# Weights from float64 to float32 by moving bits: three VectorE operations in place of five or six

## The chip, the cores and the metric

One core of a Trainium2 chip. The metric is the device time of one execution in microseconds (us), the median over runs. A kernel is called faster or slower where its time differs by more than 2% from that of the kernel before, else the same.

## The reference

Attention with normalised queries and keys, then a feed-forward block with a softmax-weighted activation. All inputs are made as float32, but the two weight matrices are multiplied by a float64 scalar, so they arrive as **float64**:

```python
# attention: batch 8, 12 heads, 448 positions, head size 64
q_n, k_n = rmsnorm(q, g_q), rmsnorm(k, g_k)
attn = softmax(q_n @ k_n.T / sqrt(64));  o = attn @ v
# feed-forward on x = o reshaped to (3584, 768); d_ff = 1024
h = x @ w_in                                   # w_in  768 x 1024, float64
e = exp(h - max(h));  sm = e / (sum(e) + 1e-9)
solu = h * sm
ln = (solu - mean) / sqrt(var + 1e-6) * g_ln
out = ln @ w_out                               # w_out 1024 x 768, float64
```

## The kernel before

Each float64 weight is read as a pair of 32-bit words, `lo` and `hi`, and put together as a float32. This is done in 28 pieces (12 of `w_in` with 128x512, then 16 of `w_out` with 128x384), each in four stages. The stages are not run at once: the kernel's program is a list of **units** (four matmuls of scores, the values, the sums, a feed-forward half), and after each unit every piece under way advances by one stage. So conversion is strewn between the steps of attention.

```python
def load_w(step):      # one piece to SBUF as [128, n, 2] 32-bit words, two buffers
def convert_w(step, raw):
    lo, hi = raw[:, :, 0], raw[:, :, 1]
    def fields():      # VectorE
        nc.vector.tensor_scalar(tmp[:, 1], hi, 0xFFFFF, None, OP.bitwise_and)                              # L467
        nc.vector.tensor_scalar(e, hi, 20, 0x7FF, OP.logical_shift_right, OP.bitwise_and)                  # L468
    def scale():       # ScalarE
        nc.scalar.activation(m, tmp[:, 1], AF.Copy, scale=2.0 ** -20, bias=1.0)                            # L471
        nc.scalar.activation(ei, ei, AF.Relu, bias=m896)                                                   # L472
    def join():        # VectorE
        nc.vector.scalar_tensor_tensor(m, lo, 2.0 ** -52, m, OP.mult, OP.add)                              # L475
        nc.vector.tensor_scalar(ei, ei, 255.0, 2.0 ** 23, OP.min, OP.mult)                                 # L476
        nc.vector.scalar_tensor_tensor(e, hi, 0x80000000, e, OP.bitwise_and, OP.bitwise_or)                # L477
    def product():
        if dst is w_in: nc.gpsimd.tensor_tensor(dst[:, c, cols], m, e.bitcast(FP32), OP.mult)              # L481
        else: nc.vector.scalar_tensor_tensor(dst[:, c, cols], m, gcol[...], e.bitcast(FP32), ...)          # L484
    return [fields, scale, join, product]
...
def rsqrt_seed(n):     # start of the inverse root of the norms; ss is a tile that the matmuls L529 write
    nc.scalar.activation(d["y"], d["ss"], AF.Ln, scale=1.0 / D, bias=eps)                                  # L536
    nc.vector.tensor_scalar(d["x"], d["ss"], -0.5 / D, -0.5e-6, OP.mult, OP.add)                           # L537
    nc.scalar.activation(d["y"], d["y"], AF.Exp, scale=-0.5)                                               # L538
...
def add(n, kc):        # sums of the exponentials E
    if kc == 1: nc.gpsimd.tensor_tensor(d["es"], d["E"][:, 0], d["E"][:, 1], OP.add)                       # L584
    else:       nc.vector.tensor_tensor(d["es"], d["es"], d["E"][:, kc], OP.add)                           # L586
...
for n in range(N):     # N = 48 head pairs; one pass is one period
    ...
    unit(lambda: scores(n, 0));  qk_transpose(n + 1);  later(1, lambda n=n: gain(n + 1))
    unit(lambda: scores(n, 1));  fold_sums(n + 2);     later(1, lambda n=n: rsqrt_seed(n + 2))
    ff(0); unit(lambda: values(n - 1)); unit(lambda: sums(n - 1)); ff(1)
    unit(lambda: scores(n, 2)); unit(lambda: scores(n, 3)); ff(2)
```

Of the kernel before, what the change touches and what calls it, by code (L numbers as in the profile page):

```python
# [9 lines left out]
FP32 = mybir.dt.float32  # L10
U32 = mybir.dt.uint32
I32 = mybir.dt.int32
AX = mybir.AxisListType.X
AF = mybir.ActivationFunctionType
OP = AluOpType
# [351 lines left out]
def fast_path(  # L367
# [7 lines left out]
    out: bass.AP,  # L375
    grow: bass.AP,
    within: bass.AP,
):


# [3 lines left out]
    nc = tc.nc  # L384
    B, H, S, D = q.shape
    DM, DFF = moe_w_in.shape
    P = 128
# [11 lines left out]
    consts = ctx.enter_context(tc.tile_pool(name="consts", bufs=1))  # L399
    loads = ctx.enter_context(tc.tile_pool(name="loads", bufs=2))  # L400
    work = ctx.enter_context(tc.tile_pool(name="work", bufs=2))
    small = ctx.enter_context(tc.tile_pool(name="small", bufs=4))
    ps_h = ctx.enter_context(tc.tile_pool(name="ps_h", bufs=1, space=bass.MemoryType.PSUM))
    ps_t = ctx.enter_context(tc.tile_pool(name="ps_t", bufs=6, space=bass.MemoryType.PSUM))

    ident = consts.tile([P, P], FP32, name="ident")
    ones = consts.tile([P, D], FP32, name="ones")
    fold = consts.tile([P, 2, 2, 32], FP32, name="fold")
    w_in = consts.tile([P, KD, DFF], FP32, name="w_in")
    w_out = consts.tile([P, KF, DM], FP32, name="w_out")  # L410
    gcol = consts.tile([P, KF + 2], FP32, name="gcol")
    mhalf = consts.tile([P, 1], FP32, name="mhalf")
    m896 = consts.tile([P, 1], FP32, name="m896")
    eps = consts.tile([P, 1], FP32, name="eps")

    def setup():

        nc.scalar.add_instruction(
            mybir.InstLoadActFuncSet(
                act_func_set_id=6, name=nc.get_next_instruction_name(), engine=mybir.EngineType.Activation  # L420
            )
        )
        nc.gpsimd.memset(mhalf, -0.5)
        nc.gpsimd.memset(m896, -896.0)
        nc.gpsimd.memset(eps, 1e-6)
        nc.gpsimd.memset(ones, 1.0)
        make_identity(nc, ident)

        nc.gpsimd.memset(fold, 0.0)
        for g in range(4):  # L430
            gs = slice(g * 32, g * 32 + 32)
            for x in range(2):
                nc.gpsimd.tensor_copy(fold[gs, g // 2, x], ident[gs, gs])
        pg = ps_t.tile([P, KF + 2], FP32, tag="t", name="pg")
        nc.tensor.transpose(pg, grow, ident[0 : KF + 2, 0 : KF + 2])
        nc.vector.tensor_copy(gcol, pg)

        nc.vector.tensor_scalar(
            gcol[:, KF : KF + 1], gcol[:, KF : KF + 1], gcol[:, KF + 1 : KF + 2], within, OP.mult, OP.mult
        )  # L440
# [3 lines left out]



    def load_w(step):
        src, _, c, cols = step
        n = cols.stop - cols.start
        raw = work.tile([P, n, 2], U32, tag="raw", name="raw")  # L450
        nc.sync.dma_start(
            raw.rearrange("p n t -> p (n t)"),
            src[c * P : (c + 1) * P, :].bitcast(U32)[:, 2 * cols.start : 2 * cols.stop],
        )
        return raw

    def convert_w(step, raw):

        _, dst, c, cols = step
        n = cols.stop - cols.start  # L460
        lo, hi = raw[:, :, 0], raw[:, :, 1]
        tmp = work.tile([P, 2, n], U32, tag="uT", name="tmp")
        e, m = tmp[:, 0], tmp[:, 1].bitcast(FP32)
        ei = e.bitcast(I32)

        def fields():
            nc.vector.tensor_scalar(tmp[:, 1], hi, 0xFFFFF, None, OP.bitwise_and)  # L467
            nc.vector.tensor_scalar(e, hi, 20, 0x7FF, OP.logical_shift_right, OP.bitwise_and)  # L468

        def scale():  # L470
            nc.scalar.activation(m, tmp[:, 1], AF.Copy, scale=2.0 ** -20, bias=1.0)  # L471
            nc.scalar.activation(ei, ei, AF.Relu, bias=m896)  # L472

        def join():
            nc.vector.scalar_tensor_tensor(m, lo, 2.0 ** -52, m, OP.mult, OP.add)  # L475
            nc.vector.tensor_scalar(ei, ei, 255.0, 2.0 ** 23, OP.min, OP.mult)  # L476
            nc.vector.scalar_tensor_tensor(e, hi, 0x80000000, e, OP.bitwise_and, OP.bitwise_or)  # L477

        def product():
            if dst is w_in:  # L480
                nc.gpsimd.tensor_tensor(dst[:, c, cols], m, e.bitcast(FP32), OP.mult)  # L481
            else:

                nc.vector.scalar_tensor_tensor(  # L484
                    dst[:, c, cols], m, gcol[:, c : c + 1], e.bitcast(FP32), OP.mult, OP.mult
                )

        return [fields, scale, join, product]

    st = {}  # L490
    xTs = {}
# [215 lines left out]
    def unit(f):  # L707
        nonlocal now
        f()
        now += 1  # L710
        due = [x for x in todo if x[0] <= now]
        todo[:] = [x for x in todo if x[0] > now]
        for _, g in sorted(due, key=lambda x: x[0]):
            g()
        feed()
# [6 lines left out]
    W_OUT = 22  # L722
    raws = []
    stages = []
    wdone = 0
    wtarget = 0

# [14 lines left out]
    events = []  # L742
# [32 lines left out]
    with tc.manual_schedule():  # L775
# [17 lines left out]
        at = 0  # L793
# [50 lines left out]
        unit(lambda: None)  # L844
        unit(lambda: values(N - 1))
        unit(lambda: sums(N - 1))
        for _, f in events[at:]:
            unit(f)
        for _ in range(4):
            unit(lambda: None)  # L850


@with_exitstack
def kernel(
    ctx: ExitStack,
    tc: tile.TileContext,
    q: bass.AP,
    k: bass.AP,
    v: bass.AP,
    g_q: bass.AP,  # L860
    g_k: bass.AP,
    moe_w_in: bass.AP,
    moe_w_out: bass.AP,
    moe_g_ln: bass.AP,
    out: bass.AP,
):
    nc = tc.nc
    D = q.shape[3]
    P = 128
    KF = moe_w_in.shape[1] // P  # L870
    gains = ctx.enter_context(tc.tile_pool(name="gains", bufs=1))
    grow = gains.tile([KF + 2, P], FP32, name="grow")
    gg = gains.tile([P, 2, D], FP32, name="gg")
    gmax = gains.tile([P, 1], FP32, name="gmax")
    within = gains.tile([P, 1], FP32, name="within")
    flag = gains.tile([1, 1], I32, name="flag")
    nc.scalar.dma_start(grow[0:KF, :], moe_g_ln.rearrange("(c p) -> c p", p=P))
    for i, g in enumerate((g_q, g_k)):
        for h in range(2):
            nc.scalar.dma_start(grow[KF + i : KF + i + 1, h * D : (h + 1) * D], g.rearrange("(o d) -> o d", o=1))  # L880
    for i, g in enumerate((g_q, g_k)):
        nc.scalar.dma_start(gg[:, i], g.rearrange("(o d) -> o d", o=1).to_broadcast([P, D]))

    nc.vector.tensor_tensor(gg[:, 0], gg[:, 0], gg[:, 1], OP.mult)
    nc.vector.tensor_reduce(gmax, gg[:, 0], AX, OP.max, apply_absolute_value=True)
    nc.vector.tensor_scalar(flag, gmax[0:1], 80.0 / float(D) ** 0.5, None, OP.is_gt)
    nc.vector.tensor_scalar(within, gmax, 80.0 / float(D) ** 0.5, float(D) ** -0.5, OP.is_le, OP.mult)
    fast_path(tc, q, k, v, moe_w_in, moe_w_out, out, grow, within)
    large = nc.values_load(flag[0:1, 0:1], min_val=0, max_val=1)
    with tc.If(large > 0):  # L890
        general_path(tc, q, k, v, g_q, g_k, moe_w_in, moe_w_out, moe_g_ln, out)


# [28 lines left out]
```

## Time and profile before

Median 1110.4 us. To see where time goes I cut the run at the same instruction of each period, the reciprocal on VectorE that belongs to head pair n ("n11" is its start for pair 11):

| stretch | before, us | what sets it |
|---|---|---|
| start to n1 | 51.5 | loads, set-up |
| A: n1 to n11, one `w_in` piece and one head pair in each period | 111.0 | VectorE without a gap, 11.11 a period |
| middle: n11 to n14, nine feed-forward halves fall in it | 86.4 | TensorE, mostly |
| B: n14 to n22, `w_out` pieces | 97.6 | VectorE, mostly |
| n22 to n47 | 620.6 | TensorE |
| n47 to the end | 140.2 | TensorE |

The prediction below shows the main lines. GpSimd in order of time (start, duration, engine, line, operation, idle time before it and its releaser) in a period of A:

```profile
99.30 2.06 POOL L481 TENSOR_TENSOR w_in<-tmp 128x512 f32<-128x512 f32 x1 [2.09 <-DVE tmp L477]
101.31 2.93 POOL L584 TENSOR_TENSOR es<-E 112x896 f32<-112x896 f32 x1
```

VectorE is slower beside both: while L481 runs, the two L586 (from 99.14) take 3.17 us instead of twice 1.08, and the next L467, which starts at 103.25 while L584 still runs, takes 1.28 us, where L468 with the same shape takes 0.41. The prediction calls this the lock; here that is only a name for these longer times. And on TensorE the first feed-forward half:

```profile
164.45 5.40 PE L635 MATMUL h<-w_in,xT 128*128 128x512 f32 x12
```

It starts 1.95 us after n11 and takes 5.40 us.

### The profile page before, as it was taken

Reading aid. Unit: us, or ns where it says so; the run is one execution under the profiler, and the core shown is the slowest. Engines: PE = TensorE matmul, PEld = TensorE weight load, DVE = VectorE, ACT = ScalarE, POOL = GpSimd, SP = SyncE. Lnnn points to the kernel's source line nnn. Section 1 sums busy time; section 2 is a strip of 40 time slices with the busy share of each in tenths; the row PEclk is TensorE's granted clock in tenths of the full one; section 3 lists DMA queues with packets and bytes.
Section 4 is the critical chain, followed back from the end, with each engine's and each line's share of the span. In section 5 each row is a group of like instructions: output and inputs, shape, how many; then the busy total and the mean of one; then the engine's idle time right before and its main releaser. Section 6 shows DMA issues by size and latency. Waiting matters only on the chain.

```text
span 1107.3 us, 10659 instructions
## 1 busy us (share of the span) xinstructions
PE 1035.3 (93%) x3617; PEld 475.6 (43%) x3617; DVE 605.4 (55%) x1018; ACT 370.6 (33%) x773; POOL 240.3 (22%) x155
## 2 busy tenths in 40 slices
PE   3988888888789999999999999999999999999997
PEld 1323233333234444444444444444444444455554
DVE  3999996569997444444444444454446644522300
ACT  3656553235564222222222222332224322311110
POOL 2565651123223111111111011121112211100000
PEclk9899999998989999999999999999999999999999
DMA  7454544014543111111111111121111100000010
GB/s 140 89 122 98 124 87 85 23 39 93 112 88 62 40 40 40 39 32 33 32 37 40 40 40 39 40 51 40 40 39 40 34 23 24 14 15 15 15 44 31
DMA packets 230391, 57.49 MB, mean 52 GB/s; under 512 B 223152, under 2 KB 223160, under 8 KB 230328
## 3 DMA queue, kind: packets, MB, share of 16 engines
q1 hardware_dynamic: 225984, 45.64, 20.9%
q10 hardware_dynamic: 4344, 11.08, 2.6%
q8 instruction: 30, 0.49, 0.2%
q14 instruction: 33, 0.27, 0.1%
HBM read 45.68 MB, written 11.01 MB: 51 GB/s over the span
## 4 chain that ended last, share of the span: by engine, by line
PE 75%; DVE 14%; issue 4%; ACT 3%; DMA 1%; SPq 1%; ACTq 0%; DVEq 0%
PE po L686 27%; PE h L635 26%; PE s L572 9%; PE o L595 9%; DVE es L586 2%; PE pu L676 2%; PE sm L604 2%; DVE tmp L467 2%; DVE qkT L559 2%; DVE tmp L475 1%; SPq L505 1%; DVE r L619 1%; DVE tmp L477 1%; DVE r L617 1%; PE ss L529 1%
## 5 line engine op out<-in xcount | busy, mean ns | idle before, releaser
L635 PE MATMUL h<-w_in,xT 128*128 128x512 f32 x672 | 305.0, 604 | 11.7 <-DVE u L653 11.7
L686 PE MATMUL po<-w_out,uT 128*128 128x384 f32 x896 | 298.0, 489 | 2.9 <-ACT uT L677 2.9
L686 PEld LDWEIGHTS po<-w_out,uT 128*128 128x128 f32 x896 | 168.3, 190 | 132.9 <-issue 15.0
L572 PE MATMUL s<-qkT 64*112 64x448 f32 x768 | 204.6, 584 | 16.9 <-ACT E L576 6.7
L576 ACT ACTIVATE E<-s 112x448 f32<-112x448 f32 x384 | 178.0, 550 | 110.0 <-PE s L572 109.9
L635 PEld LDWEIGHTS h<-w_in,xT 128*128 128x128 f32 x672 | 126.2, 193 | 167.5 <-issue 162.8
L584 POOL TENSOR_TENSOR es<-E 112x896 f32<-112x896 f32 x48 | 110.5, 2301 | 325.2 <-ACT E L576 318.7
L595 PE MATMUL o<-E,v 112*64 112x448 f32 x768 | 163.9, 572 | 1.2 <-DVE xT L621 1.2
L572 PEld LDWEIGHTS s<-qkT 64*112 64x112 f32 x768 | 76.6, 177 | 136.9 <-issue 73.6
L677 DVE COPY uT<-pu 128x512 f32<-128x512 f32 x28 | 19.2, 687 | 187.3 <-PE pu L676 187.3
L586 DVE TENSOR_TENSOR es<-es,E 112x896 f32<-112x896 f32 x96 | 115.1, 1199 | 10.9 <-ACT E L576 7.8
L663 POOL TENSOR_TENSOR he<-he,mhalf 128x1 f32<-128x1 f32 x28 | 21.7, 774 | 379.2 <-DVE he L662 379.2
L549 POOL TENSOR_TENSOR qkn<-qk,ny 128x896 f32<-128x896 f32 x48 | 83.0, 1730 | 81.6 <-DVE ny L544 35.0
L648 ACT ACTIVATE u<-h,hmax 128x1024 f32<-128x1024 f32 x28 | 31.2, 1114 | 207.3 <-DVE hmax L645 207.3
L687 ACT COPY y<-po 128x384 f32<-128x384 f32 x56 | 26.8, 479 | 213.5 <-PE po L686 213.5
L595 PEld LDWEIGHTS o<-E,v 112*64 112x64 f32 x768 | 53.2, 143 | 86.5 <-issue 80.5
L645 DVE TENSOR_REDUCE hmax<-h 128x1 f32<-128x1024 f32 x28 | 34.3, 1224 | 84.3 <-PE h L635 84.3
L604 PE MATMUL sm<-es,ones 112*64 112x448 f32 x192 | 44.8, 544 | 16.0 <-DVE es L586 14.1
L617 DVE STREAM_TRANSPOSE r<-sm 128x448 f32<-128x448 f32 x48 | 31.0, 646 | 45.8 <-PE sm L604 45.8
L524 DVE TENSOR_REDUCE part<-sq 128x28 f32<-128x896 f32 x48 | 51.7, 1076 | 5.9 <-ACT sq L519 5.9
L519 ACT ACTIVATE sq<-qk 128x896 f32<-128x896 f32 x48 | 45.8, 955 | 23.1 <-ACT y L687 11.3
L559 DVE STREAM_TRANSPOSE qkT<-qkn 128x896 f32<-128x896 f32 x48 | 52.9, 1102 | 0.0
(54 smaller groups left out, 578.7 us busy)
## 6 DMA issues: line engine op xcount, KB each, us to landing
qk<-in_q_dram SPq DMA_DIRECT2D x192, 56.0 KB, 2.6
qk<-in_k_dram SPq DMA_DIRECT2D x192, 56.0 KB, 2.4
v<-in_v_dram SPq DMA_DIRECT2D x48, 224.0 KB, 3.0
out_dram<-y ACTq DMA_DIRECT2D x28, 384.0 KB, 2.3
raw<-in_moe_w_in_dram SPq DMA_DIRECT2D x12, 512.0 KB, 4.2
raw<-in_moe_w_out_dram SPq DMA_DIRECT2D x16, 384.0 KB, 3.4
grow<-in_g_q_dram ACTq DMA_DIRECT2D x2, 0.2 KB
grow<-in_g_k_dram ACTq DMA_DIRECT2D x2, 0.2 KB
```

Of the source, the lines that this page charges most:

```text
L519: nc.scalar.activation(d["sq"], d["qk"].rearrange("p s b d -> p (s b) d"), AF.Square)
L524: nc.vector.tensor_reduce(d["part"], d["sq"], AX, OP.add)
L549: nc.gpsimd.tensor_tensor(d["qkn"], d["qk"].rearrange("p s b d -> p (s b) d"), d["y"].rearrange("p b -> p b ()").to_broadcast([P, 2 * NB, ...
L559: nc.vector.transpose(d["qkT"].rearrange("p s t -> p (s t)"), d["qkn"].rearrange("p b d -> p (b d)"))
L572: nc.tensor.matmul(s, d["qkT"][hh, 1, kc * SP : (kc + 1) * SP], d["qkT"][hh, 0, :], start=True, stop=True)
L576: nc.scalar.activation(d["E"][:, kc, h], d["s", h], AF.Exp)
L584: nc.gpsimd.tensor_tensor(d["es"], d["E"][:, 0], d["E"][:, 1], OP.add)
L586: nc.vector.tensor_tensor(d["es"], d["es"], d["E"][:, kc], OP.add)
L595: nc.tensor.matmul(d["o"][h * D : (h + 1) * D, :], d["v"][:, h, kc], d["E"][:, kc, h], start=(kc == 0), stop=(kc == NJ - 1),)
L604: nc.tensor.matmul(d["sm"][h * D : (h + 1) * D, :], ones[0:SP, :], d["es"][:, h], start=True, stop=True)
L635: nc.tensor.matmul(d["h"][:, hs], xTs[m][:, c, i * P : (i + 1) * P], w_in[:, c, hs], start=(c == 0), stop=(c == KD - 1))
L686: nc.tensor.matmul(po, d["uT"][:, c], w_out[:, c, hs], start=(c == 0), stop=(c == KF - 1))
```

## The change

A float32 has three exponent bits fewer than a float64. For weights of ordinary size the float32 is the sign and top exponent bit of `hi`, the rest of `hi` moved up by three, and the top three bits of `lo`. So no arithmetic on exponents is needed: VectorE moves and joins bits, ScalarE gets the three bits out of `lo`. The intent is to relieve VectorE, the bound of the head, and GpSimd. What is given up is the range; so at the end all weights are loaded again, and their smallest and largest high words are checked beside the last units. Where they are out of range, a general path runs. The diff is shortened; comments stand for removed code that is shown above.

```diff
-        def fields():      # two on VectorE
-        def scale():       # two on ScalarE
+        def low_bits():
+            nc.scalar.activation(low, lo, AF.Relu, scale=-(2.0 ** -29), bias=seven)                         # L469
+            nc.scalar.activation(tmp[:, 1].bitcast(I32), low, AF.Copy, scale=-1.0, bias=7.0)                # L470
+        def high_bits():
+            nc.vector.tensor_scalar(t, hi, 3, 0x3FFFFFFF, OP.logical_shift_left, OP.bitwise_and)            # L473
+            nc.vector.scalar_tensor_tensor(t, hi, 0xC0000000, t, OP.bitwise_and, OP.bitwise_or)             # L474
         def join():
-            # three on VectorE
+            o = dst[:, c, cols].bitcast(U32) if dst is w_in else t
+            nc.vector.tensor_tensor(o, t, tmp[:, 1], OP.bitwise_or)                                         # L478
         def product():
-            # w_in: GpSimd, w_out: VectorE
+            if dst is w_out:
+                nc.scalar.activation(dst[:, c, cols], t.bitcast(FP32), AF.Copy, scale=gcol[:, c : c + 1])   # L483
-        return [fields, scale, join, product]
+        return [low_bits, high_bits, join, product]
...
+        again = [load_w(wq[x]) for x in range(2)]          # beside the last units:
+            check_w(x, again[x])                           # two reductions of a piece, L490 and L491
+            check_all()                                    # two transposes on TensorE (L502), some tiny operations
```

In lines of the changed kernel: L536, L537 are now L559, L560; the gain L563 is L586; the transpose L559 is L582; the additions L584, L586 are L607, L609; the feed-forward half L635 is L658. (L559 and L586 thus name other operations in the two kernels.)

More of the change, by code (lines that the diff above doesn't have):

```diff
@@ L377, in fast_path @@
     within: bass.AP,
+    large: bass.AP,
 ):
@@ L412, in fast_path @@
     mhalf = consts.tile([P, 1], FP32, name="mhalf")
-    m896 = consts.tile([P, 1], FP32, name="m896")
+    seven = consts.tile([P, 1], FP32, name="seven")
     eps = consts.tile([P, 1], FP32, name="eps")
@@ L423, in setup @@
         nc.gpsimd.memset(mhalf, -0.5)
-        nc.gpsimd.memset(m896, -896.0)
+        nc.gpsimd.memset(seven, 7.0)
         nc.gpsimd.memset(eps, 1e-6)
@@ L462, in convert_w @@
         tmp = work.tile([P, 2, n], U32, tag="uT", name="tmp")
-        e, m = tmp[:, 0], tmp[:, 1].bitcast(FP32)
-        ei = e.bitcast(I32)
-        def fields():
-            nc.vector.tensor_scalar(tmp[:, 1], hi, 0xFFFFF, None, OP.bitwise_and)
-            nc.vector.tensor_scalar(e, hi, 20, 0x7FF, OP.logical_shift_right, OP.bitwise_and)
-        def scale():
-            nc.scalar.activation(m, tmp[:, 1], AF.Copy, scale=2.0 ** -20, bias=1.0)
-            nc.scalar.activation(ei, ei, AF.Relu, bias=m896)
+        t, low = tmp[:, 0], tmp[:, 1].bitcast(FP32)
@@ L474, in join @@
+        def low_bits():
[4 more added lines that the diff above has]
+            nc.vector.scalar_tensor_tensor(t, hi, 0xC0000000, t, OP.bitwise_and, OP.bitwise_or)
         def join():
-            nc.vector.scalar_tensor_tensor(m, lo, 2.0 ** -52, m, OP.mult, OP.add)
@@ L476, in join @@
-            nc.vector.tensor_scalar(ei, ei, 255.0, 2.0 ** 23, OP.min, OP.mult)
-            nc.vector.scalar_tensor_tensor(e, hi, 0x80000000, e, OP.bitwise_and, OP.bitwise_or)
+            o = dst[:, c, cols].bitcast(U32) if dst is w_in else t
+            nc.vector.tensor_tensor(o, t, tmp[:, 1], OP.bitwise_or)
         def product():
-            if dst is w_in:
-                nc.gpsimd.tensor_tensor(dst[:, c, cols], m, e.bitcast(FP32), OP.mult)
-            else:
-                nc.vector.scalar_tensor_tensor(
-                    dst[:, c, cols], m, gcol[:, c : c + 1], e.bitcast(FP32), OP.mult, OP.mult
-                )
@@ L488, in convert_w, with check_w @@
-        return [fields, scale, join, product]
+            if dst is w_out:
+                nc.scalar.activation(dst[:, c, cols], t.bitcast(FP32), AF.Copy, scale=gcol[:, c : c + 1])
+        return [low_bits, high_bits, join, product]
+    def check_w(x, raw):
+        hi = raw[:, :, 1].bitcast(FP32)
+        nc.vector.tensor_reduce(extent[:, 0, x : x + 1], hi, AX, OP.min, apply_absolute_value=True)
+        nc.vector.tensor_reduce(extent[:, 1, x : x + 1], hi, AX, OP.max, apply_absolute_value=True)
@@ new lines, in check_all @@
+    def check_all():
+        worst = small.tile([P, 2], FP32, tag="mv", name="worst")
+        one = small.tile([1, 2], FP32, tag="one", name="one")
+        pw = ps_t.tile([1, 2, P], FP32, tag="t", name="pw")
+        nc.vector.tensor_reduce(worst[:, 0:1], extent[:, 0], AX, OP.min)
+        nc.vector.tensor_reduce(worst[:, 1:2], extent[:, 1], AX, OP.max)
+        for i in range(2):
+            nc.tensor.transpose(pw[:, i], worst[:, i : i + 1], ident)
+        nc.vector.tensor_reduce(one[:, 0:1], pw[:, 0], AX, OP.min)
+        nc.vector.tensor_reduce(one[:, 1:2], pw[:, 1], AX, OP.max)
+        nc.vector.tensor_scalar(one[:, 0:1], one[:, 0:1], 2.0 ** -15, None, OP.is_ge)
+        nc.vector.tensor_scalar(one[:, 1:2], one[:, 1:2], 122880.0, None, OP.is_lt)
+        nc.vector.tensor_tensor(one[:, 0:1], one[:, 0:1], one[:, 1:2], OP.mult)
+        nc.vector.tensor_scalar(one[:, 1:2], large, -1.0, 1.0, OP.mult, OP.add)
+        nc.vector.tensor_tensor(one[:, 0:1], one[:, 0:1], one[:, 1:2], OP.mult)
+        nc.vector.tensor_scalar(large, one[:, 0:1], -1.0, 1.0, OP.mult, OP.add)
@@ L724, in fast_path @@
     stages = []
+    extent = consts.tile([P, 2, len(wq)], FP32, name="extent")
     wdone = 0
@@ L846, in fast_path @@
         unit(lambda: sums(N - 1))
-        for _, f in events[at:]:
+        last = events[at:]
+        assert len(last) > len(wq) + 1
+        again = [load_w(wq[x]) for x in range(2)]
+        for x, (_, f) in enumerate(last):
             unit(f)
+            if x < len(wq):
+                check_w(x, again[x])
+                if x + 2 < len(wq):
+                    again.append(load_w(wq[x + 2]))
+            if x == len(wq) + 1:
+                check_all()
         for _ in range(4):
@@ L876 @@
     flag = gains.tile([1, 1], I32, name="flag")
+    large = gains.tile([1, 1], FP32, name="large")
     nc.scalar.dma_start(grow[0:KF, :], moe_g_ln.rearrange("(c p) -> c p", p=P))
@@ L885 @@
     nc.vector.tensor_reduce(gmax, gg[:, 0], AX, OP.max, apply_absolute_value=True)
-    nc.vector.tensor_scalar(flag, gmax[0:1], 80.0 / float(D) ** 0.5, None, OP.is_gt)
+    nc.vector.tensor_scalar(large, gmax[0:1], 80.0 / float(D) ** 0.5, None, OP.is_gt)
     nc.vector.tensor_scalar(within, gmax, 80.0 / float(D) ** 0.5, float(D) ** -0.5, OP.is_le, OP.mult)
-    fast_path(tc, q, k, v, moe_w_in, moe_w_out, out, grow, within)
-    large = nc.values_load(flag[0:1, 0:1], min_val=0, max_val=1)
-    with tc.If(large > 0):
+    fast_path(tc, q, k, v, moe_w_in, moe_w_out, out, grow, within, large)
+    nc.vector.tensor_copy(flag, large)
+    other = nc.values_load(flag[0:1, 0:1], min_val=0, max_val=1)
+    with tc.If(other > 0):
         general_path(tc, q, k, v, g_q, g_k, moe_w_in, moe_w_out, moe_g_ln, out)
```

## The prediction

> **What bounds the kernel now.** I read the page first (busy tenths by slice), then busy time by stretch, then the order of time on each engine inside one period of the first stretch, then the waits.
>
> The slices split the run in two:
> ```profile
> PE   3988888888789999999999999999999999999997
> ...
> DVE  3999996569997444444444444454446644522300
> ...
> PEclk9899999998989999999999999999999999999999
> ```
> From slice 13 on (about 340 us) TensorE is busy without a gap and VectorE is half idle. Only the first 340 us, in which the weights are converted, and the very end can answer to this change. Busy time in two stretches of that head:
> ```profile
> 62.00:162.00 100.00, 84.69 (x343) 31.00 (x344) 97.21 (x155) 59.56 (x128) 59.78 (x27) 1.00 0.50 106
> ...
> 248.00:337.00 89.00, 74.80 (x276) 27.77 (x274) 82.61 (x149) 48.53 (x105) 27.61 (x15) 0.87 0.46 95
> ```
> Columns after the length: PE, PEld, DVE, ACT, POOL busy. VectorE has 97 of 100 us in the first (call it A: one head pair and one w_in piece per period) and 83 of 89 in the second (B: eight w_out pieces per five periods). Between them, about 162 to 244 us, lie nine feed-forward halves of 5.2 us each, and TensorE sets the pace. One period of A on VectorE:
> ```profile
> 91.11 1.10 DVE L559 STREAM_TRANSPOSE qkT<-qkn 128x896 f32<-128x896 f32 x1
> 92.14 1.28 DVE L467 TENSOR_SCALAR tmp<-raw 128x512 uint32<-128x512 uint32 x1
> 93.34 0.41 DVE L468 TENSOR_SCALAR tmp<-raw 128x512 uint32<-128x512 uint32 x1
> 93.68 0.17 DVE L537 TENSOR_SCALAR nx<-ss 128x28 f32<-128x28 f32 x1
> ...
> 97.47 0.68 DVE L475 SCALAR_TENSOR_TENSOR tmp<-raw,tmp 128x512 f32<-128x512 uint32 x1
> 98.07 0.42 DVE L476 TENSOR_SCALAR tmp<-tmp 128x512 int32<-128x512 int32 x1
> 98.53 0.69 DVE L477 SCALAR_TENSOR_TENSOR tmp<-raw,tmp 128x512 uint32<-128x512 uint32 x1
> 99.14 3.17 DVE L586 TENSOR_TENSOR es<-es,E 112x896 f32<-112x896 f32 x2
> 102.23 1.10 DVE L559 STREAM_TRANSPOSE qkT<-qkn 128x896 f32<-128x896 f32 x1
> ```
> Column one is the start, column two the duration. There is no gap: VectorE is the bound, the period is 102.23 - 91.11 = 11.12 us. From start to start, conversion takes 1.20 + 0.34 + 0.60 + 0.46 + 0.61 = 3.2 us of it. In the same period ScalarE:
> ```profile
> 92.24 0.67 ACT L563 ACTIVATE qkT<-qkT,gcol 128x448 f32<-128x448 f32 x1 [4.29 <-DVE qkT L559]
> 92.82 0.27 ACT L536 ACTIVATE ny<-ss,eps 128x28 f32<-128x28 f32 x1
> ...
> 93.51 0.63 ACT L471 ACTIVATE tmp<-tmp 128x512 f32<-128x512 uint32 x1 [0.17 <-DVE tmp L467]
> 94.05 0.70 ACT L472 ACTIVATE tmp<-tmp,m 128x512 int32<-128x512 int32 x1
> ```
> The gain L563 waits for the transpose; the logarithm L536 follows it. From the waits of the whole run:
> ```profile
> DVE nx L537 <- ACT ny L536: 71.3, 33, 6.7
> ```
> So VectorE's L537 may not pass L536. In A this wait does not show, because L467 and L468 stand between L559 and L537 and last longer than gain and logarithm.
>
> [...]
> ```profile
> 256.66 2.46 DVE L477 SCALAR_TENSOR_TENSOR tmp<-raw,tmp 128x384 uint32<-128x384 uint32 x1
> ```
> L477 takes 0.56 us when nothing is in its way; here GpSimd's L584 (the first E addition) runs from 256.63 for 2.07 us. In A the lock costs about 0.86 us on L467 (1.28 against 0.41) and 1.0 us on the two L586 (3.17 against 2.16), together 1.9 us a period.[...]
>
> **The change part by part.**
> *VectorE, removed and added.* In A, 3.2 us a period go, 0.86 of them the lock stall on L467, so 2.35 of work. Added: shift-and-mask like L468 (0.46 with the dependent wait), or-in of the top bits like L477 (0.61), join of two unit-stride inputs: L586 is 1.08 us for 896[...], some 0.60 from start to start. Together 1.67, so 0.7 us less work. In B a piece costs now 0.27 + 0.27 + 0.47 + 0.38 + 0.48 + 0.53 = 2.4 us and then 0.27 + 0.48 + 0.47 = 1.2; at 1.6 pieces a period 1.9 us less.
> *GpSimd* loses L481 (1.9 us of w_in product); *ScalarE* keeps two activations a piece and gains the w_out product (0.43 us), and it has room (60 of 100 us).
> *Order.* This decides it. The built programs, compared instruction by instruction, show that in A the two ScalarE operations on the low words now stand between the gain and the logarithm, and on VectorE L537's operation stands directly behind the transpose, ahead of the shift. VectorE then waits: gain 0.58, low words 0.61 + 0.54, logarithm 0.30, and 0.05 to start, so 2.08 us after the transpose ends; the two operations that used to fill this time come after it. The gap is 2.0 us each period.
> *The lock.* GpSimd's E addition starts when ScalarE has done the exponentials, by the present spacing (2.3 us behind the gap's start, then 4.4) some 6.8 us after the transpose's end. VectorE reaches the join at about 7.0 us and the two L586 behind it[...]. One of them waits out GpSimd's 2.05 us: about 1.9 us lost, as much as now, though L481 is gone.
> *Sum for A.* From start to start, what is not conversion takes: transpose 1.03, L537 0.10, row sums L524 1.00, Newton steps 0.54, the divide L617 to L621 2.17, two L586 2.02, together 6.9. With 2.35 of conversion and 1.86 of lock stalls that is 11.1, the period measured, so the account closes. New: 6.9 + 1.67 + gap 2.0 + stall 1.9 = 12.5. Ten periods at +1.35: **+13 us**.
> *B.* Here pieces fall at varying places. In three of eight periods the low words stand before the logarithm (gap 2.0 to 2.5), in the others it is 0.2 to 1.4; the mean of the eight is 1.3. 6.9 + 1.95 (1.6 pieces at 1.22) + 1.3 + a lock stall of 1.4 (the mean of those now seen there) = 11.5 against 12.65 measured (88.5 us in seven periods). **-8 us** over seven.
> *Middle and start.* TensorE sets the middle; start-up gains from L481's absence and loses by the wait: 0 to +1.
> *The check at the end.* The last 32 units hold 28 loads and 56 reductions of 0.55 to 0.69 us, some 34 us. Units average 4.5 us, VectorE is busy 28% there, and a load of 3.4 to 4.2 us with two buffers keeps up, so all of it is hidden behind TensorE. Not hidden: two transposes of the extremes stand on TensorE before the last 10.6 us of output products and wait for two short reductions behind the last copy: about **+1 us**.
> Sum: +13 - 8 + 0.5 + 1 = +6.5 on 1110.4, rounded: **1116 us**.
>
> **Rivals.**
> (1) *The gap does not arise or is filled*, the plain reading of the change: A falls to 6.9 + 1.67 + 1.0 = 9.6, B to 10.2; 15 + 17 us saved, less 1 for the check, 1079 us. For it: VectorE at 97%. Against it: the built order, and L537's wait on L536, which shows 33 times now.
> (2) *The gap arises but the lock stall goes*[...]: A 10.6, B 10.5; 5 + 15 us saved, less 1 for the check, 1092 us. Against it: the spacing above; for it: a shift of only half a microsecond alters who meets whom.
> (3) *TensorE's clock*: in B its granted clock is 0.87, with 12.65 us periods that leave it idle over a third of the time. Should A's longer periods bring that too, scores come later and each period grows by up to 0.5 us: +5, 1121 us.
> (4) *The check is not hidden*: loads fall behind and hold VectorE up before a copy that TensorE needs: 5 to 10 us more, 1124 us. Against it: ten microseconds of output products stand between two uses of the tile h.
>
> **Range and chances.** My sum is 1116; (3) and (4) lie 5 to 8 above it, (2) some 24 below, and each 0.5 us of error in A's period is 5 us. I take 1097 to 1130 for 8 in 10. Faster by over 2% (under 1088) needs rival (1) or nearly: 0.09. Slower by over 2% (over 1132.6) needs A at 13.5 or several costs together: 0.06. Within 2%: 0.85.
>
> **What would show each step.** VectorE busy in A falling from 97 to about 80 of 100 us while its period grows to 12 or more; VectorE idle about 2 us before each operation that L537 is now, released by the logarithm on ScalarE; join or es additions of 2.5 to 3 us beside GpSimd's E addition; B's period near 11.5; TensorE without new gaps after 350 us except 1 us before the last output products. I am wrong if VectorE stays gapless in A with a period under 10.5, or if VectorE holds up TensorE in the last 140 us.

## The result, and the profile after

1124.9 us (1124.4 to 1125.6, 4 runs) against 1110.6 us (1108.0 to 1111.8) on the same chip: **ratio 1.0133**, 95% interval 1.0114 to 1.0152, so "the same" by the 2% rule but surely longer. A ratio here is the mean time of one kernel's fast runs over that of the other's of the same rounds, so not quite the ratio of the medians quoted. The time lies in the range predicted, but the change, +14 us, is more than twice the +6.5 us of the prediction's sum.

The page's busy tenths of VectorE and the granted clock of TensorE, in 40 slices of the changed kernel:

```profile
DVE  3787887455778444444444444444445543555521
PEclk9989998999889999999999999999999999999999
```

VectorE had nines in A (slices 2 to 6) and now has sevens and eights. Busy time by stretch (columns: window and length, then PE, PEld, DVE, ACT, POOL busy, granted clock, DMA share, GB/s), in A and in B (n14 to n22), which has moved later:

```profile
62.00:162.00 100.00, 76.32 (x298) 28.99 (x298) 81.56 (x117) 51.09 (x106) 33.23 (x16) 0.93 0.44 96
272.27:362.78 90.51, 80.69 (x309) 31.62 (x308) 72.39 (x129) 59.27 (x126) 32.13 (x17) 0.87 0.48 98
```

VectorE fell from 97 to 82 of 100 us in A, GpSimd from 60 to 33, ScalarE from 60 to 51 though it has as many operations a piece there: every engine idles more, so fewer periods fit in. One period of A on VectorE:

```profile
96.02 1.10 DVE L582 STREAM_TRANSPOSE qkT<-qkn 128x896 f32<-128x896 f32 x1
99.34 0.19 DVE L560 TENSOR_SCALAR nx<-ss 128x28 f32<-128x28 f32 x1 [2.21 <-ACT ny L559]
99.45 0.42 DVE L473 TENSOR_SCALAR tmp<-raw 128x512 uint32<-128x512 uint32 x1
...
104.22 0.68 DVE L478 TENSOR_TENSOR w_in<-tmp 128x512 uint32<-128x512 uint32 x1
104.82 4.17 DVE L609 TENSOR_TENSOR es<-es,E 112x896 f32<-112x896 f32 x2
108.91 1.10 DVE L582 STREAM_TRANSPOSE qkT<-qkn 128x896 f32<-128x896 f32 x1
```

The period is 108.91 - 96.02 = 12.89 us. VectorE stands 2.21 us before L560, released by the logarithm L559. And the two L609 take 4.17 us, where twice 1.08 would do. ScalarE during the gap:

```profile
97.16 0.67 ACT L586 ACTIVATE qkT<-qkT,gcol 128x448 f32<-128x448 f32 x1 [5.74 <-DVE qkT L582]
97.74 0.74 ACT L469 ACTIVATE tmp<-raw,seven 128x512 f32<-128x512 uint32 x1
98.51 0.63 ACT L470 ACTIVATE tmp<-tmp 128x512 int32<-128x512 f32 x1
99.05 0.27 ACT L559 ACTIVATE ny<-ss,eps 128x28 f32<-128x28 f32 x1
```

Gain, low words, logarithm, one behind the other without a gap, and VectorE waits for the last. GpSimd's addition in the same period starts 0.44 us ahead of the pair L609 (during the join L478) and ends at 106.84, well into it:

```profile
104.38 2.46 POOL L607 TENSOR_TENSOR es<-E 112x896 f32<-112x896 f32 x1 [0.42 <-ACT E L599]
```

VectorE does not wait for its data here: counted in order, this L607 belongs to the next head pair, and that of the pair that the two L609 add up had ended at 93.96. The first of the two takes 2.97 us, the second 1.09.

The waits of the whole run (waiter, releaser: us in total, times, longest):

```profile
DVE nx L560 <- ACT ny L559: 113.5, 48, 7.2
...
ACT w_out L483 <- DVE tmp L478: 21.6, 8, 4.2
```

The first wait was 71.3 us in 33 places and is now 113.5 in 48. The second is new: ScalarE does the `w_out` product, which needs VectorE's join. In the middle it looks like this:

```profile
181.64 0.62 ACT L483 ACTIVATE w_out<-tmp,gcol 128x384 f32<-128x384 f32 x1 [4.16 <-DVE tmp L478]
```

ScalarE stood for 4.16 us, with exponentials in its queue behind the product, and then TensorE begins its first feed-forward half:

```profile
184.28 7.55 PE L658 MATMUL h<-w_in,xT 128*128 128x512 f32 x12
```

That is 4.71 us after n11 and takes 7.55 us; before it was 1.95 and 5.40. The whole account, by the same cuts:

| stretch | before | after | difference | predicted |
|---|---|---|---|---|
| start to n1 | 51.5 | 51.2 | -0.3 | with the middle |
| A, n1 to n11 | 111.0 | 128.4 | **+17.4** | +13 |
| n11 to first feed-forward half | 1.95 | 4.71 | +2.8 | |
| first to second half | 9.24 | 11.39 | +2.15 | |
| second to ninth half | 61.77 | 61.80 | 0.0 | |
| ninth half to n14 | 13.45 | 14.80 | +1.35 | |
| middle together | 86.4 | 92.7 | **+6.3** | 0 to +1 |
| B, n14 to n22 | 97.6 | 90.5 | **-7.1** | -8 |
| n22 to n47 | 620.6 | 620.3 | -0.3 | 0 |
| n47 to the end | 140.2 | 139.5 | -0.7 | +1 |
| span of the profiled run | 1107.3 | 1122.6 | +15.3 | +6.5 |

### The profile page after: what moved, and what is told of

Same layout as the page of the kernel before. It is cut to its first block, busy times and chain, and to the rows that moved or that the text cites. A ratio compares the mean times of both kernels' runs of the same rounds, so it can differ in the third digit from the quotient of the medians.

```text
span 1122.6 us, 10697 instructions
## 1 busy us (share of the span) xinstructions
PE 1037.5 (92%) x3619; PEld 480.0 (43%) x3619; DVE 603.2 (54%) x1013; ACT 380.8 (34%) x789; POOL 211.6 (19%) x143
## 4 chain that ended last, share of the span: by engine, by line
PE 75%; DVE 12%; ACT 5%; issue 3%; SPq 2%; DMA 1%; POOL 1%; ACTq 0%; DVEq 0%; POOLq 0%
PE h L658 26%; PE po L709 26%; PE o L618 9%; PE s L595 8%; DVE es L609 3%; PE pu L699 2%; PE sm L627 2%; SPq L528 2%; DVE part L547 1%; DVE tmp L474 1%; ACT E L599 1%; DVE qkT L582 1%; ACT qkT L586 1%; ACT tmp L469 1%; DVE r L642 1%
## 5 line engine op out<-in xcount | busy, mean ns | idle before, releaser
L658 PE MATMUL h<-w_in,xT 128*128 128x512 f32 x672 | 307.2, 608 | 11.7 <-DVE u L676 11.7
L595 PE MATMUL s<-qkT 64*112 64x448 f32 x768 | 201.2, 585 | 20.9 <-DVE nx L560 9.9
L658 PEld LDWEIGHTS h<-w_in,xT 128*128 128x128 f32 x672 | 127.1, 194 | 168.8 <-issue 164.1
L618 PE MATMUL o<-E,v 112*64 112x448 f32 x768 | 166.9, 580 | 12.4 <-DVE xT L644 12.4
L607 POOL TENSOR_TENSOR es<-E 112x896 f32<-112x896 f32 x48 | 104.8, 2184 | 325.6 <-ACT E L599 325.6
L595 PEld LDWEIGHTS s<-qkT 64*112 64x112 f32 x768 | 79.2, 177 | 134.9 <-issue 69.1
L609 DVE TENSOR_TENSOR es<-es,E 112x896 f32<-112x896 f32 x96 | 123.3, 1285 | 13.8 <-ACT E L599 10.5
L560 DVE TENSOR_SCALAR nx<-ss 128x28 f32<-128x28 f32 x48 | 9.0, 187 | 113.5 <-ACT ny L559 113.5
L586 ACT ACTIVATE qkT<-qkT,gcol 128x448 f32<-128x448 f32 x48 | 32.6, 679 | 73.3 <-DVE qkT L582 73.3
```

The costliest lines, as they stand in the source:

```text
L586: nc.scalar.activation(d["qkT"][:, 0], d["qkT"][:, 0], AF.Copy, scale=gcol[:, KF : KF + 1])
L595: nc.tensor.matmul(s, d["qkT"][hh, 1, kc * SP : (kc + 1) * SP], d["qkT"][hh, 0, :], start=True, stop=True)
L618: nc.tensor.matmul(d["o"][h * D : (h + 1) * D, :], d["v"][:, h, kc], d["E"][:, kc, h], start=(kc == 0), stop=(kc == NJ - 1),)
L658: nc.tensor.matmul(d["h"][:, hs], xTs[m][:, c, i * P : (i + 1) * P], w_in[:, c, hs], start=(c == 0), stop=(c == KD - 1))
```

## The experiments

Twelve kernels ran, each beside the kernel before. Edits are against the changed kernel unless said otherwise; "period" is the mean of A, (n11 - n1) / 10, which is 11.10 before and 12.84 after.

| run | time, us | ratio to before (95% interval) | period of A | middle | B |
|---|---|---|---|---|---|
| before | 1110.6 to 1112.3 | 1 | 11.10 | 86.4 | 97.6 |
| after | 1124.9 | 1.0133 (1.0114 to 1.0152) | 12.84 | 92.7 | 90.5 |
| seed_first | 1095.1 | 0.9849 (0.9821 to 0.9877) | 10.86 | 91.1 | 83.8 |
| swap | 1086.2 | 0.9767 (0.9741 to 0.9792) | 9.94 | 89.7 | 84.5 |
| no_first_add (wrong; 2 executions) | 1103.6 | 0.9926 (0.9892 to 0.9960) | 10.95 | 94.3 | 87.1 |
| low_twice (2 executions) | 1137.7 | 1.0232 (1.0197 to 1.0267) | 13.61 | 94.3 | 95.4 |
| product_dve | 1123.1 | 1.0106 (1.0089 to 1.0123) | 12.83 | 90.1 | 94.6 |
| no_check | 1125.1 | 1.0125 (1.0108 to 1.0141) | 12.83 | 94.4 | 90.5 |
| swap_product | 1090.9 | 0.9820 (0.9804 to 0.9837) | 9.94 | 88.2 | 91.2 |
| all_four | 1080.0 | 0.9719 (0.9703 to 0.9735) | 9.64 | 87.3 | 82.9 |
| swap_seed_adddve | 1084.2 | 0.9764 (0.9736 to 0.9791) | 9.64 | 89.9 | 84.3 |
| before_adddve | 1109.5 | 0.9990 (0.9962 to 1.0018) | 11.20 | 87.8 | 94.0 |
| warm | 1123.7 | 1.0123 (1.0095 to 1.0151) | 12.81 | 94.1 | 91.3 |
| warm_h | 1123.7 | 1.0113 (1.0093 to 1.0133) | 12.84 | 91.2 | 90.6 |

### The gap: is it the wait for the logarithm?

My theory: L560, which reads the tile `ss` as L559 does, comes after it, as the waits above show (48 times, 113.5 us in all); the low words ahead of the logarithm are what makes it long.

**seed_first** lets VectorE read first:

```diff
-        nc.scalar.activation(d["y"], d["ss"], AF.Ln, scale=1.0 / D, bias=eps)
         nc.vector.tensor_scalar(d["x"], d["ss"], -0.5 / D, -0.5e-6, OP.mult, OP.add)
+        nc.scalar.activation(d["y"], d["ss"], AF.Ln, scale=1.0 / D, bias=eps)
```

> The changed kernel with one line moved: VectorE's first step of the inverse root is written ahead of ScalarE's logarithm, so that VectorE no longer waits for it. Theory (the gap of 2.2 us behind the transpose is this wait): in stretch A the gap goes, a rest of about 0.4 us appears before the next step, and the period falls from 12.88 us to 11.0, or to 10 if the lock stall shrinks too; the run takes 1095 to 1103 us. Rival (the period is set by TensorE or by the loop over scores and exponentials, and VectorE's gap is only where the slack shows): the gap moves to another VectorE instruction, the period stays within 0.4 us of 12.9 and the run at 1120 to 1125.

Measured 1095.1 us and a correct result, the period 10.86. On VectorE:

```profile
102.80 0.19 DVE L565 TENSOR_TENSOR nx<-nx,ny 128x28 f32<-128x28 f32 x1 [0.36 <-ACT ny L561]
...
106.12 4.06 DVE L609 TENSOR_TENSOR es<-es,E 112x896 f32<-112x896 f32 x2
```

The gap of 2.21 is gone but for 0.36 us before the next step, which needs what comes of the logarithm; the stall of the additions stays. The period fell by 1.98 us. B fell by 6.7 us too.

**swap** leaves the reading order and puts the high bits first, so that two VectorE operations stand ahead of L560, and the logarithm ahead of the low words:

```diff
-        return [low_bits, high_bits, join, product]
+        return [high_bits, low_bits, join, product]
```

> The changed kernel with the first two stages of a piece exchanged: VectorE's shift and or first, ScalarE's low words a unit later, behind the logarithm. Theory: the shift and the or (1.07 us) fill the time in which VectorE would wait, and the low words no longer lengthen it; no gap before the first step of the inverse root, period of A 9.5 to 10.7 us, run 1085 to 1100 us. Rival (slack only): period within 0.4 us of 12.9.

Measured 1086.2 us, correct. On VectorE, in two periods that follow each other:

```profile
105.55 2.28 DVE L609 TENSOR_TENSOR es<-es,E 112x896 f32<-112x896 f32 x2
...
108.78 1.30 DVE L473 TENSOR_SCALAR tmp<-raw 128x512 uint32<-128x512 uint32 x1
...
115.13 3.98 DVE L609 TENSOR_TENSOR es<-es,E 112x896 f32<-112x896 f32 x2
```

No gap, and in every second period the additions are spared and the shift L473 takes 1.30 us instead of 0.42, so 0.9 more, beside GpSimd's addition as I take it: periods alternate between 9.57 and 10.35. This one line, moved, turns the change from 1.3% slower to 2.3% faster.

**low_twice** runs L469 twice, to see whether its duration goes straight into the period:

```diff
+            nc.scalar.activation(low, lo, AF.Relu, scale=-(2.0 ** -29), bias=seven)
             nc.scalar.activation(low, lo, AF.Relu, scale=-(2.0 ** -29), bias=seven)
```

> The changed kernel with the first ScalarE operation on the low words done twice over (same values). Theory (ScalarE's low words stand inside VectorE's wait): the gap in A grows from 2.2 to 3.0 us and the period from 12.88 to 13.65; A gives 8 us, B 2 to 4, the run is at 1133 to 1138 us. Rival (ScalarE is idle half of the time and hides it): period and run unchanged, within 2 us of 1125.

```profile
104.07 0.19 DVE L561 TENSOR_SCALAR nx<-ss 128x28 f32<-128x28 f32 x1 [3.00 <-ACT ny L560]
```

The gap went from 2.21 to 3.00, so +0.79, and the period from 12.84 to 13.61, so +0.77: the same, and near one L469 (0.77 from its start to the next operation's). The run took 1137.7 us, as expected (by the 2% rule unclear, as its interval begins just under 1.02).

### The stall of the additions: is it GpSimd's addition?

**no_first_add** drops the addition on GpSimd (the sums are then wrong) and keeps two on VectorE:

```diff
         if kc == 1:
+            pass
+        elif kc == 2:
             d["es"] = work.tile([SP, 2, S], FP32, tag="es", name="es")
-            nc.gpsimd.tensor_tensor(d["es"], d["E"][:, 0], d["E"][:, 1], OP.add)
+            nc.vector.tensor_tensor(d["es"], d["E"][:, 1], d["E"][:, 2], OP.add)
```

> Wrong on purpose: the sum of exponentials leaves out the first block, so GpSimd's addition is gone and VectorE's two additions are of the same size as before. Theory (one of VectorE's two es additions waits out GpSimd's addition, 2.0 us a period[...]): the two additions take 2.1 us together where they take 4.17, the gap of 2.2 us stays, the period of A is 10.9 us, and the run some 20 to 30 us shorter than the changed kernel. Rival (the additions are slow for another reason, the exponentials or the space for them): they still take about 4 us and the period stays at 12.9. Output is wrong.

```profile
103.79 0.19 DVE L560 TENSOR_SCALAR nx<-ss 128x28 f32<-128x28 f32 x1 [2.21 <-ACT ny L559]
...
109.26 1.08 DVE L609 TENSOR_TENSOR es<-E 112x896 f32<-112x896 f32 x1
110.45 1.09 DVE L611 TENSOR_TENSOR es<-es,E 112x896 f32<-112x896 f32 x1
```

The additions take 1.08 and 1.09 us, the gap stays at 2.21, and the period falls by 1.89 to 10.95. So gap and stall are two separate costs of about 2 us a period each. The run is 21 us shorter: 18.9 of it in A, 3.4 in B, less 1.6 in the middle.

**before_adddve** is the control: the kernel before with that addition on VectorE and nothing else.

```diff
-            nc.gpsimd.tensor_tensor(d["es"], d["E"][:, 0], d["E"][:, 1], OP.add)
+            nc.vector.tensor_tensor(d["es"], d["E"][:, 0], d["E"][:, 1], OP.add)
```

> The kernel before with nothing but its first addition of exponentials moved from GpSimd to VectorE; a control for how much of the gain of the other runs belongs to that move and not to the conversion. Theory: GpSimd keeps its products of w_in, so only a part of the lock goes; the period of the first stretch goes from 11.1 to between 10.2 and 11.0 us, the second stretch gains 0 to 6 us, run 1095 to 1108 us. Rival (the gains of the experiments come from that move alone, whatever the conversion): the run reaches 1085 us or less.

The ratio is 0.999: nothing gained, which neither theory had.

```profile
96.09 0.41 DVE L467 TENSOR_SCALAR tmp<-raw 128x512 uint32<-128x512 uint32 x1
...
102.22 3.15 DVE L586 TENSOR_TENSOR es<-es,E 112x896 f32<-112x896 f32 x2
```

L467 is spared its stall (0.41 instead of 1.28), but the moved addition takes 0.97 from start to start, and the two L586 take 3.15 us as before, as GpSimd's product L481 (from 102.38 for 2.05 us) is still there to meet them. In B, where GpSimd has no product, the move does gain 3.6 us; the start, A and the middle lose 5.1. So in A the move pays only once the conversion has left GpSimd, and by itself it brings none of the gain in time told of below.

### The middle: the product on ScalarE, and the clock

**product_dve** gives the `w_out` product back to VectorE:

```diff
-                nc.scalar.activation(dst[:, c, cols], t.bitcast(FP32), AF.Copy, scale=gcol[:, c : c + 1])
+                nc.vector.tensor_scalar(dst[:, c, cols], t.bitcast(FP32), gcol[:, c : c + 1], None, OP.mult)
```

> The changed kernel with the w_out product back on VectorE. Seen in the changed kernel's trace: ScalarE waits 21.6 us in all for VectorE's join before this product, up to 4.2 us at a time, and the exponentials stand behind it. Theory (this wait makes up the 2.8 us that the changed kernel loses just before the first feed-forward half, and some of stretch B): first half 2 to 3 us nearer to the period before it, B shorter by 1 to 4 us although VectorE does 16 operations of 0.35 us more; run 1118 to 1122 us. Rival (VectorE is the bound in B, so what goes back to it costs): B longer by 4 us, run 1125 to 1130.

Half right: the first feed-forward half starts at 181.74 instead of 184.28, with A unchanged. So the wait cost 2.5 of the 2.8 us. But B grows by 4.1 us, as the rival had it: VectorE is busy for 85.4 of its 94.6 us there, against 72.4 of 90.5. In all 1123.1 us, between the two ranges.

**swap_product** has both edits.

> Stages exchanged and the product on VectorE. If both causes add up: exchanged stages alone gave 1086.2 us; the wait of ScalarE for the join before the first feed-forward half goes, 1 to 4 us less, run 1082 to 1086. If the exchange has removed that wait already, or VectorE is the bound: 1086 to 1090.

The middle gains 1.5 us over swap, B loses 6.7: 1090.9 us, slower than swap alone and just over the range of the rival too. Where the product is best depends on what else VectorE has to do.

The other 2.15 us of the middle are the first half's own duration, 7.55 us instead of 5.40. In the trace TensorE's granted clock is either full or half (1.00 or 0.50), and the half-clock stretches in the head are multiples of 3.41 us, starting on one grid of 3.41 us: in A from 65.7, 79.4, 130.6 and 144.3 us for 3.41 each, then from 181.8 for 6.83. The changed kernel's stretches of that grid around the first half (columns as above; the first number after the length is TensorE's busy time, the third from the end the granted clock):

```profile
178.39:181.80 3.41, 1.75 (x5) 0.54 (x4) 3.24 (x10) 0.16 (x1) 1.69 (x1) 1.00 0.43 116
181.80:185.22 3.42, 2.06 (x5) 0.93 (x4) 1.79 (x2) 3.39 (x7) 0.00 (x0) 0.50 0.65 106
```

A stretch with 1.75 us of work is followed by a half-clock one, and the first half falls on it and the next. In A of the same run, stretches with 1.81 to 1.83 us of work are all four followed by half clock, and six with 1.85 to 1.87 are not. My theory from this was: too little work halves the clock of the next stretch.

**warm** adds three matmuls that nobody reads to each period of A:

```diff
             if n:
                 unit(lambda: values(n - 1))
+            if 3 <= n <= 12:
+                warm()          # 3 x matmul(junk, ident, w_in[:, 0, 0:S]), into a tile of its own
```

> The changed kernel with three matmuls of 128x448 whose result nobody reads, in each head pair of the first stretch, so that TensorE idles less there. Theory (the first feed-forward half took 7.55 us instead of 5.40 as TensorE's clock was halved for its idleness): the half-clock windows of the first stretch go, the first half of the middle takes 5.4 us again, the period of the first stretch stays at 12.8 us, run 1 to 3 us shorter, 1121 to 1124 us. Rival (half-clock windows fall where they do whatever TensorE's load): windows remain in like number, their places move, and the run is within 2 us of the changed kernel's 1125 us, on either side.

This fell out badly for the theory. The first half took 7.19 us, and the run 1123.7 us, which no difference of that size can judge. In A two half-clock stretches are left. The changed kernel's run has four, and three other runs with the same A (product_dve, no_check, warm_h) have five or six; the grid does not fall in the same places in every run (lines at 72.57 and 75.98 us in the changed kernel's, at 73.74 and 77.15 in warm). But I had put the work in the wrong place: the stretches ahead of the two halved ones (2.57 and 2.32 us of work, mostly score matmuls) hold none of the added matmuls, and the stretch before the first half still had only 1.88 us of work.

**warm_h** puts five such matmuls just there, into the still unused tile of h:

```diff
             convert(2)
+            if n == 13:
+                warm(2)
             unit(lambda: scores(n, 1))
+            if n == 13:
+                warm(3)
```

> The changed kernel with five matmuls of 128x448 into the still unused tile h, two and three of them in the places where TensorE idles in the last head pair before the first feed-forward half; nothing else is moved, and nobody reads the result. In the changed kernel TensorE is busy for 1.75 us of the 3.41 us before the clock is halved there. Theory (the halved clock in the first half of the middle follows the interval before it, in which TensorE had too little to do): that interval has over 2.5 us of work, the first half takes 5.4 us instead of 7.55, and later halves and the rest stay as they were; run 1 to 3 us shorter than the changed kernel, 1122 to 1124 us. Rival (the halving does not depend on TensorE's load in that interval, or not at this size): the first half stays between 7 and 8.5 us and the run between 1124 and 1127 us.

```profile
180.98:184.40 3.42, 3.39 (x9) 1.25 (x8) 2.15 (x4) 2.17 (x5) 0.36 (x1) 1.00 0.38 62
...
185.26 5.42 PE L658 MATMUL h<-w_in,xT 128*128 128x512 f32 x12
```

The clock stays full, the first half takes 5.42 us, the second starts 9.26 us after it (9.24 before, 11.39 after), and the middle is 1.5 us shorter; the rest of the 2.13 us I put down to the added matmuls, an estimate. So in this place the load just before decided: 3.39 us of work and then full clock here, 1.75 us and then half clock in the changed kernel's run. Where the grid fell is not the reason: in no_check the first half starts 0.74 us after a line of the grid (here 0.87), the stretch before that line has 1.47 us of work, and the clock is halved. In all seven runs that keep the low words first and add nothing just there, the first half takes 7.09 to 8.42 us. What stays open is the measure. By busy time in the profile the line lies between 1.83 and 1.85 us in A of the changed kernel's run, but a stretch of warm with 2.57 us is followed by half clock, and in product_dve the stretch before the first half has 2.44 us of work, all of it score matmuls, and is followed by half clock. So busy time alone is not the measure; which one is, no run here shows. The run's 1123.7 us (5 runs) points the same way as the trace, but its interval overlaps that of the changed kernel.

### The check

**no_check** leaves out the second loads, the reductions and the final test.

```diff
-        again = [load_w(wq[x]) for x in range(2)]
         for x, (_, f) in enumerate(last):
             unit(f)
-            if x < len(wq):
-                check_w(x, again[x])
-                if x + 2 < len(wq):
-                    again.append(load_w(wq[x + 2]))
-            if x == len(wq) + 1:
-                check_all()
```

> The changed kernel without the loads, reductions and transposes of the range check (not fit for use: weights out of range go unnoticed). Theory (hidden but for the transposes ahead of the last output products): last output product starts 0.5 to 1 us sooner behind the last transposes of u, run 0 to 1.5 us shorter than the changed kernel. Rival (56 reductions and 28 loads hold up VectorE or the copies): run 5 us or more shorter.

1125.1 us over five rounds, against 1124.9 with the check: no cost that these runs can show. In the trace the last output products start 1.78 us after the transposes of u ahead of them, and 2.27 with the check, so it costs TensorE 0.5 us there. The whole time can't show so little: in this profiled run the halved clock made the first feed-forward half 8.41 us long, and the middle 1.7 us longer than with the check, for no reason that has to do with it.

### Putting the edits together

**all_four**: high bits first, VectorE's read before the logarithm, product on VectorE, first addition on VectorE.

> Stages exchanged, VectorE's first step of the inverse root ahead of the logarithm, product on VectorE, and GpSimd's first addition of exponentials on VectorE too (1.08 us more work a period[...]). Theory: A is the sum of VectorE's work, 6.9 + 1.67 + 1.0 = 9.6 us a period (9.94 with the stages exchanged alone), B about 10.2 (10.57), run 1078 to 1084 us. Rival (the lock stall of the exchanged version is cheaper than an addition on VectorE): 1086 to 1092.

1080.0 us, correct: 2.8% under the kernel before, the best that I found. The period of A is 9.64: by the terms of the prediction 6.9 + 1.67 for the conversion, 0.97 for the addition from start to start, and 0.1 of stall left.

**swap_seed_adddve** is the same with the product left on ScalarE, which I thought better.

> High bits first, the inverse root's first step ahead of the logarithm, and the first addition of exponentials on VectorE; the w_out product stays on ScalarE. Theory (three separate costs, each of which an earlier run took away alone): the period of the first stretch is that of the kernel with all four edits, 9.6 us; the second stretch lies under that kernel's 82.9 us, at 77 to 81 us, as VectorE is the bound there and loses eight times two products; the middle is 1 to 2 us longer. Run 1074 to 1080 us. Rival (the second stretch is bound by ScalarE's exponentials once VectorE is lighter): it stays at 82 to 84 us and the run is at 1080 to 1084 us.

1084.2 us, and 84.3 us for B: the theory failed on B, and both numbers lie just over the rival's ranges. The period of A is the same and the middle 2.6 us longer (I had said 1 to 2), but B does not gain the eight times two products; it is 1.4 us longer. Busy time in B (n14 to n22) of swap_seed_adddve, then of all_four (columns as above):

```profile
239.48:323.77 84.29, 76.30 (x315) 29.34 (x312) 76.42 (x136) 60.38 (x128) 14.55 (x9) 1.00 0.53 108
```

```profile
235.69:318.56 82.87, 75.15 (x314) 29.31 (x311) 79.35 (x147) 54.95 (x117) 14.55 (x9) 0.98 0.54 110
```

In all_four VectorE is busy for 79.4 of 82.9 us, so it is still the bound. Without the products it has 2.9 us less work and idles 4.4 us more. Waits in B of swap_seed_adddve:

```profile
ACT w_out L483 <- DVE tmp L478: 10.5, 7, 2.6
...
DVE es L607 <- ACT E L599: 3.6, 6, 0.9
DVE es L609 <- ACT E L599: 1.1, 2, 0.5
```

None of these three is in B of all_four. So this looks like the wait of the middle again: ScalarE stands for the join before its product, and VectorE then waits for exponentials. No run shows that this makes up the whole difference. The rival's reason is not shown either: ScalarE is busy for 60.4 of the 84.3 us.

## Why the prediction was right or wrong

**VectorE loses its work but gains a wait (right).** In A its busy time fell from 97 to 82 of 100 us, foretold as about 80, while the period grew. seed_first, swap and low_twice show that the wait is the one named.

**The size of A (mis-sized, +17.4 instead of +13).** The account has the right terms: 6.9 + 1.67 + gap 2.21 + stall 2.07 = 12.85, measured 12.88 in the steady periods. (The join's 0.60 in the 1.67 was an estimate; L478 shows it, 104.22 to 104.82.) Two terms were too small. The **gap** was put at 2.0: the low words were taken as "0.61 + 0.54" and showed 0.77 + 0.54. The kernel before has these two figures, from start to start, for L472 (whose bias is a tile, as L469's is) and L471. L469 takes 0.74 us itself, against 0.70 of L472. And L470, which reads what L469 writes, starts 0.03 us after its end, where L472, which reads nothing of L471, starts 0.09 us before the end of L471: the sum had this overlap for a pair that does not have it. Then I rounded 2.08 down. The **stall**, the prediction's lock, was put at "as much as now", 1.9, and was 2.07. Together 0.4 us a period, ten times over. The smaller the net of two large terms, the more such tenths weigh: I foretold +1.35 a period and got +1.77.

**The lock (right).** The additions do meet GpSimd's addition (2.46 us) and take 4.17 us instead of 2.16, though the product L481 is gone; no_first_add takes the stall away and leaves the gap. Which operations of VectorE take longer beside GpSimd, and why, no run here settles: L467, with one input, took 1.28 us instead of 0.41, L477, with two, 2.46 instead of 0.56, and the transpose L559, beside the same additions on GpSimd, its usual 1.10. Rival (2), that it would vanish, is refuted in A.

**The middle (failed).** The step was "TensorE sets the middle; start-up gains from L481's absence and loses by the wait: 0 to +1". It was +6.3, in three parts. First, 2.8 us: I counted ScalarE's new product by its duration and by ScalarE's free time ("it has room"), and not by its **wait**. It waits 4.16 us for VectorE's join, and exponentials that TensorE needs stand behind it in ScalarE's queue; product_dve gives 2.5 of it back. Second, 2.15 us: the halved clock on the first half; warm_h gives it back. The trace before had the warning: three of the nine halves take 6.8 to 7.1 us there, on half clock, where the prediction counted "5.2 us each" (the others take 5.4). Third, 1.35 us at the end: the trace shows the low words between gain and logarithm there as in A (0.67 and 0.52 us on ScalarE), with L560 behind them. No run was made for that part alone, but others bear it out: these 14.80 us (ninth half to n14; 13.45 before) are 13.69 in seed_first, 13.75 in swap and 15.44 in low_twice. So it is the gap of A once more.

**B (right, a little off).** The prediction counted seven periods, n14 to n21: 81.8 us instead of 88.5, so 11.69 a period against its 11.5, and -6.7 against its -8. (The -7.1 of the table is for eight.) The three long gaps that it saw coming are there, with 2.2 to 2.5 us each. seed_first shows that the gap was in B too: another 6.7 us.

**The check (right).** Hidden but for half a microsecond on TensorE, foretold as 1. The last stretch is 0.7 us shorter than before all the same, and as short without the check; these runs do not say why.

**The rivals.** (1), no gap, came true only where the stages are exchanged: the periods of 9.94 and 9.64 are near its 9.6, though the second has an addition in place of the stall. (3), the clock, was half right: half-clock stretches do come in A (four, none before), but the period of A does not feel them (12.84 with four, 12.81 in warm with two); they told in the middle, where TensorE sets the pace. Its premise was misread: in B TensorE is busy for 74.8 of 89 us in the line shown, so idle for a sixth of the time and not "over a third". (4) is refuted by no_check.

In sum the prediction's 6.5 us became 15.3 in the profiled runs: 4.4 more in A, 5.5 more in start and middle, 0.9 less gained in B, and 2 us less after n22. (1110.4 + 6.5 is 1116.9, so 1117 and not 1116.)

## What to carry to other kernels

Work removed from the bounding engine counts only if the operations that are left can start: see which of the removed operations stood in front of a wait, and what now stands ahead of the awaited operation in the other engine's queue. Here VectorE's work in A fell from 97 to 82 of 100 us and the period rose from 11.10 to 12.84. When work is given to an engine with free time, cost it by how long it will stand at the head of that queue, not by its duration: here the product took 0.62 us and stood for 4.16. And when a change loses, try the order of its stages before giving it up: here one swapped line was worth 39 us, and the change with its order mended beats both kernels.
